# Eleven blocks of three heads, GpSimd scaling, a fixed SyncE order and a new pacing in a fused attention and gated-MLP kernel

## The chip, the cores and the metric

The kernel runs on one core of a Trainium2 chip. The metric is the device time of one execution in microseconds (us); less is better. The engines are called as the profile calls them: PE (TensorE matmul), PEld (its weight loads), DVE (VectorE), ACT (ScalarE), POOL (GpSimd) and SP (SyncE, which here only issues DMAs). Every engine works through its own instructions in a fixed order and waits on semaphores for the others.

## The reference

Input `x` has 2048 rows of 640; there are 32 heads of 20 features. All matrices are bfloat16.

```python
xn = layernorm(x)
# A: linear attention with learned softmax features
q, k, v = heads(xn @ wqkv)                     # 32 heads of 20
pq, pk = q @ w_phi, k @ w_phi                  # per head, 20 x 20
phi_q = concat(softmax(pq), softmax(-pq))      # 40 features, phi_k alike
kv = phi_k^T @ v                               # per head, summed over all rows
z  = sum over rows of phi_k
o  = (phi_q @ kv) / (phi_q . z + 1e-6)
A  = merge_heads(o) @ wo
# B: gated MLP, 1536 wide
B  = (silu(xn @ w1) * (xn @ w3)) @ w2
return x + A + B
```

No query can be finished before all 2048 keys have gone into `kv`.

## The kernel before

**Tiles.** The rows are 16 tiles of 128, grouped in 4 chunks of 512. The normalised rows of a chunk are needed transposed (`xnT`): chunk 0 is transposed on PE, chunks 1 to 3 are stored to DRAM (`xnd`) and read back by a transposing DMA, both issued by SP (`LN_out`, L363 and L368). DVE makes the normalised rows in `ln_apply` (L332).

**Units of work.** `K(t)` and `Q(t)` project a tile on PE with `wkphi` or `wqphi` (two halves of five 320-column matmuls, L424, weights folded from `wqkv` and `w_phi` by `prep`). ACT takes exponentials of both signs (L472), DVE sums them per head (L481) and takes reciprocals (L494), and DVE or POOL multiplies (L499), into a tile `phi` of 10 blocks x 2 signs x 64 columns. A block holds 64 of a tile's 640 feature columns, so it touches up to four heads. `V(t)` projects values. `KV(t)` (L542) adds a tile into two accumulators with ten matmuls of 84 columns; `kv_evac` masks off the products of different heads. `GU(c, fi)` is a gate and an up product for 128 of the 1536 MLP columns of one chunk: ten 512-column matmuls (L613), a tanh on ACT (L629), `gs` on DVE (L634), a copy on ACT (L652) and the product `hT` on POOL (L657). For queries, `phiq` goes to DRAM (L522), is read back transposed per pair of tiles as `pqT` (L534), meets `kv` in `RT(t)` (ten matmuls, L687), is divided on DVE (`ATT`, L716, L717, L722), stored (`od`, L741) and read back transposed per pair as `oT` (`OT`, L755). `O(t)` makes the output tile: 24 MLP matmuls (L780), ten with `wo` and `oT` (L786), the residual on DVE (L798) and the store (L803).

**What sets the order.** `Plan` is a list scheduler that runs when the kernel is built. Each unit of work has a planned duration and latency, the units it needs and the buffers it takes. PE's units keep the order in which they are written. For the other engines the planner takes, of the first 80 units waiting, the one that could start first:

```python
    k = (max(t, free.get(eng, 0.0)), o["n"])
```

The loop at L910 writes PE's order: tile after tile of keys, with `fill(us)` putting in as many `GU` units as the given time is worth, the remaining `Q` tiles after t = 11, and at the end eight rounds of two output tiles. Steps of a later chunk's `ln_apply` are tied to the `GU` units, one per unit (L895). The planner's order is handed on unit by unit, but the tile framework places instructions by its own priorities too, so what stands on an engine is shown below from the built programs.

**Names in short.** In this document GU1.11 is the last `GU` of chunk 1, K12 is `K(12)`, g3 and a3 are the MLP and the attention part of output tile 3.

Of the kernel before, what the change touches and what calls it, by code (L numbers as in the profile page):

```python
# [10 lines left out]
class Plan:  # L11
# [7 lines left out]
    def op(self, eng, dur, fn, deps=(), takes=None, frees=(), after=0.0, lat=0.0):  # L19
        o = dict(eng=eng, dur=dur, fn=fn, deps=[d for d in deps if d is not None], takes=takes,  # L20
                 frees=list(frees), after=after, lat=lat, n=len(self.ops), end=None, open=0)
        for f in o["frees"]:
            f["open"] += 1
        self.ops.append(o)
        return o
# [4 lines left out]
    def run(self):  # L30
# [20 lines left out]
        while left:  # L51
            best = None
            for eng, q in queue.items():
                for o in q[:1] if eng == "PE" or eng[0] == "a" else q[:80]:
# [3 lines left out]
                    k = (max(t, free.get(eng, 0.0)), o["n"])  # L58
# [3 lines left out]
            (t, _), o = best  # L62
            if o["takes"]:
                ring = self.rings[o["takes"]]
                ring.remove(min(ring))
# [12 lines left out]
def kernel(  # L78
# [30 lines left out]
    GH = 8  # L109
    EPS = 1e-5  # L110
    h0 = [64 * j // Dh for j in range(10)]
# [18 lines left out]
    pq_d = [dram.tile([256, 2 * D], bf, name=f"pqd{i}") for i in range(NST // 2)]  # L130
# [16 lines left out]
    kvm = acts.tile([P, 10, 4, Dh + 1], bf, name="kvm")  # L147
# [5 lines left out]
    def load_x(dst, t0, n, k, queue=nc.sync):  # L153
        queue.dma_start(
# [40 lines left out]
    mask = consts.tile([P, 10, 4], bf, name="mask")  # L195
# [45 lines left out]
    def kv_constants():  # L241
        for q in range(2):
            make_band(band2[64 * q : 64 * q + 64, :], 20)
        for j in range(10):
            b = 4 + 5 * h0[j] - 16 * j
            nc.gpsimd.tensor_copy(out=mask[:, j, :], in_=band2[:, b : b + 16 : 5])
# [15 lines left out]
    def act_us(n):  # L262
        return 0.075 + n / 1200.0

    def dve_us(n, x=1):
        return 0.065 + n / 960.0 / x
# [4 lines left out]
    arrive = [3.0, 3.4, 3.8, 4.2] + [19.0] * 4   # L271
# [10 lines left out]
    def ln_stats(t, k=None, parts=(0, 1)):  # L282
        c, i = divmod(t, 4)

        def fn():
# [8 lines left out]
            "DVE", 0.47 * len(parts), fn, after=arrive[t] if t < 8 else 0.0,  # L294
# [33 lines left out]
    def ln_apply(t, deps=(), k=None):  # L328
# [10 lines left out]
        apply_of[t] = plan.op("DVE", dve_us(D, 4), fn, deps=[rstd_of[t], *deps], frees=[xg_of[c]])  # L339
# [19 lines left out]
    def LN_out(c, ds):  # L359
# [3 lines left out]
            lambda: nc.sync.dma_start(out=xn_d[c][:].rearrange("(t p) d -> p t d", p=P), in_=xn[c][:]),  # L363
# [3 lines left out]
        def tr():  # L367
            pinned["xnT", c] = nc.sync.dma_start_transpose(  # L368
                out=xnT[:, :, 512 * c : 512 * c + 512], in_=xn_d[c][:]
            )  # L370

        xt = plan.op("SP", 0.5, tr, deps=[st], lat=5.0)
# [3 lines left out]
    def fetch(t, k):  # L376
# [7 lines left out]
        X_of[t] = plan.op("SP", 0.5, lambda: load_x(xg[c], i, 1, c), deps=[xg_of[c]], lat=2.5, after=30.0)  # L384
        ln_stats(t, k)
# [67 lines left out]
    def features(t, key, engines):  # L453
# [7 lines left out]
        def alp():  # L461
            box["phi"] = work.tile([P, 10, 2, 64], bf, name="phi" + key, tag="phi", bufs=5)
# [25 lines left out]
        muls = []  # L488
        for sgn, eng in enumerate(engines):

            def rec(sgn=sgn):
                if sgn == 0:
                    box["r"] = small.tile([P, 2, H], f32, name=key + "r", tag="kr", bufs=2)
                nc.vector.reciprocal(out=box["r"][:, sgn, :], in_=box["s"][:, sgn, :])  # L494

            last = plan.op("DVE", dve_us(H, 0.15), rec, deps=[last])

            def mul(sgn=sgn, eng=eng):
                ins = (nc.vector if eng == "DVE" else nc.gpsimd).tensor_mul(  # L499
                    out=box["phi"][:, :, sgn, :],  # L500
                    in0=box["e"][:, sgn, :].rearrange("p (h d) -> p h d", d=Dh),
                    in1=box["r"][:, sgn, :, None].to_broadcast([P, H, Dh]),
                )
                if key == "k" and sgn == 0:
                    pinned[t] = ins

            m = plan.op(eng, dve_us(D) if eng == "DVE" else 1.5, mul, deps=[last, pa], frees=[ea])
            if eng == "DVE":
                last = m
            muls.append(m)  # L510
        return muls, pa, box

    def K(t):
        phik_of[t], phik_a[t], _ = features(t, "k", ("DVE", "POOL"))
        pin_of[t] = phik_of[t][0]

    def Q(t, engines=("POOL", "POOL")):
# [4 lines left out]
            lambda: nc.sync.dma_start(  # L522
                out=pq_d[pair][i * P : (i + 1) * P, :], in_=box["phi"][:].rearrange("p j a f -> p (j a f)")
            ),
            deps=muls, frees=[pa], lat=2.5,
        )
        if i == 1:

            def al():
                pqT[pair] = big.tile([P, 10, 256], bf, name="pqT", tag="big")  # L530
# [3 lines left out]
                "SP", 0.5, lambda: nc.sync.dma_start_transpose(out=pqT[pair][:], in_=pq_d[pair][:]),  # L534
                deps=[pq_st[t - 1], pq_st[t], pqT_a[pair]], lat=4.5,
            )

    def KV(t):
        def fn():
            for j in (0, 5, 1, 6, 2, 7, 3, 8, 4, 9):  # L540
                acc = (kva, kvb)[j // 5]
                nc.tensor.matmul(  # L542
                    acc[:, 84 * (j % 5) : 84 * (j % 5) + 84],
                    phik_b[t][:, j, :, :].rearrange("p a f -> p (a f)"),
                    vaug[t % 4][:, h0[j] : h0[j] + 4, :].rearrange("p h d -> p (h d)"),
                    start=(t == 0 and j % 5 == 0), stop=(t == NST - 1), skip_group_check=True,
                )

        KV_of[t] = plan.op("PE", pe_us(10, 90), fn, deps=phik_of[t] + V_of[t], frees=[phik_a[t]])
# [53 lines left out]
    def GU(c, fi, mode):  # L603
# [45 lines left out]
        else:  # L649

            def uc():
# [4 lines left out]
                "POOL", 1.3,  # L656
# [7 lines left out]
    def kv_evac():  # L664
        for half, acc in enumerate((kva, kvb)):
# [343 lines left out]
```

## Time and profile before

| | |
|---|---|
| median of 6 runs | 283.35 us (282.56 to 286.35) |
| profiled execution | 284.07 us, its span 282.3 us |
| granted TensorE clock, mean | 0.988 of full speed |
| busy: PE, DVE | 269.7 us (96%), 179.9 us (64%) |
| busy: ACT, POOL | 127.7 us (45%), 123.5 us (44%) |
| DMA | 37.06 MB, 131 GB/s over the span |

The span is what the profile covers; the time of that execution is 1.77 us longer. Busy shares are means over stages with different limits. A matmul's record overlaps the next one's, so the length of a matmul is read here from the distance between two starts and not from its own duration.

### The profile page before, as it was taken

The numbers are of one execution on the slowest core, as the hardware profiler recorded it, in microseconds if no ns is written. First come the engines' busy times: TensorE is split into PE (matmuls) and PEld (weight loads), VectorE is DVE, ScalarE is ACT, GpSimd is POOL, SyncE is SP. The second block draws the span as 40 slices with busy tenths as digits, with TensorE's granted clock in tenths as the row PEclk, the third lists the DMA queues.
The fourth block names the chain that finished last, engine by engine and source line by source line (L and its number), as shares of the span: only waits on it lengthen the run. The fifth ranks groups of instructions, "written<-read, shape, count | busy, mean of one in ns | idle before, by whom it ended". The sixth has DMA issues, their size and how long they took to land.

```text
span 282.3 us, 5148 instructions
## 1 busy us (share of the span) xinstructions
PE 269.7 (96%) x1932; PEld 166.7 (59%) x1932; DVE 179.9 (64%) x367; ACT 127.7 (45%) x285; POOL 123.5 (44%) x133
## 2 busy tenths in 40 slices
PE   7999999999999995999999939999999999999996
PEld 2545555555556564565664617765766756657775
DVE  5525899998776777589689906665574564434221
ACT  3668676666677673576774211325233251130000
POOL 6233646875475454326579703336138145040000
PEclk9999999999999999799999989999999999999999
DMA  6999828700460024105735883597623675722301
GB/s 200 296 244 303 240 96 203 262 2 0 125 156 0 2 93 97 48 0 93 212 87 162 239 199 63 153 221 208 165 95 93 142 201 122 138 52 73 93 26 46
DMA packets 68217, 37.06 MB, mean 131 GB/s; under 512 B 47584, under 2 KB 66144, under 8 KB 68192
## 3 DMA queue, kind: packets, MB, share of 16 engines
q1 hardware_dynamic: 67616, 36.37, 49.1%
q10 hardware_dynamic: 576, 0.36, 0.4%
q8 instruction: 15, 0.25, 0.4%
q14 instruction: 10, 0.08, 0.1%
HBM read 12.81 MB, written 12.45 MB: 89 GB/s over the span
## 4 chain that ended last, share of the span: by engine, by line
PE 87%; DMA 7%; issue 2%; DVE 1%; ACT 1%; SPq 1%; POOL 0%; DVEq 0%; POOLq 0%; ACTq 0%
PE bank L613 35%; PE bank L424 20%; PE bank L780 18%; PE bank L786 8%; PE rtbank L687 2%; DMA xnT<-xnd_90 2%; DMA wv<-in_A_wqkv_dram 2%; DMA oT<-od_99 1%; DMA xnd_90<-xn 1%; PE bank L570 1%; PE kva L542 1%; PE kvb L542 1%; ACT eq L472 1%; DVE gs L634 0%; POOL phik L499 0%
## 5 line engine op out<-in xcount | busy, mean ns | idle before, releaser
L657 POOL TENSOR_TENSOR hT<-gs,up 128x512 bf16<-128x512 bf16 x48 | 55.2, 1156 | 59.7 <-ACT up L652 28.0
L424 PEld LDWEIGHTS <-xnT 128*128 128x128 bf16 x480 | 46.4, 99 | 25.1 <-DMA xnT<-xnd_90 3.0
L613 PE MATMUL bank<-xnT,w_108 128*128 128x512 bf16 x240 | 60.1, 379 | 0.0
L613 PE MATMUL bank<-xnT,w_107 128*128 128x512 bf16 x240 | 60.1, 380 | 0.0
L780 PE MATMUL bank<-w_109,hT 128*128 128x320 bf16 (+2 forms) x396 | 57.6, 295 | 0.0
L499 POOL TENSOR_TENSOR phiq<-eq,qr 128x640 bf16<-128x640 bf16 x27 | 34.2, 1284 | 50.6 <-issue 17.6
L634 DVE SCALAR_TENSOR_TENSOR gs<-th,bank 128x512 bf16<-128x512 bf16 x48 | 32.1, 671 | 21.4 <-ACT th L629 19.9
L780 PEld LDWEIGHTS <-hT 128*128 128x128 bf16 x396 | 37.3, 98 | 14.0
L472 ACT ACTIVATE eq<-bank 128x320 bf16<-128x320 f32 x64 | 23.0, 439 | 49.4 <-PE bank L424 49.4
L629 ACT ACTIVATE th<-bank 128x512 bf16<-128x512 f32 x48 | 28.8, 599 | 30.6 <-PE bank L613 30.2
L652 ACT ACTIVATE up<-bank 128x512 bf16<-128x512 f32 x48 | 28.7, 597 | 26.1 <-PE bank L613 25.0
L613 PEld LDWEIGHTS <-w_108 128*128 128x128 bf16 x240 | 23.2, 98 | 27.3
L613 PEld LDWEIGHTS <-w_107 128*128 128x128 bf16 x240 | 23.3, 98 | 22.9 <-issue 0.3
L481 DVE TENSOR_REDUCE qs<-eq 128x64 f32<-128x1280 bf16 x16 | 23.7, 1481 | 18.8 <-ACT eq L472 18.8
L798 DVE TENSOR_TENSOR res<-bank,xr 128x320 bf16<-128x320 f32 (+2 forms) x33 | 15.9, 482 | 30.0 <-PE bank L786 29.7
L481 DVE TENSOR_REDUCE ks<-ek 128x64 f32<-128x1280 bf16 x16 | 23.6, 1475 | 13.3 <-ACT ek L472 13.3
L786 PE MATMUL bank<-wo,oT 128*128 128x320 bf16 (+2 forms) x165 | 26.0, 305 | 4.6 <-DMA oT<-od_99 4.6
L499 POOL TENSOR_TENSOR phik<-ek,kr 128x640 bf16<-128x640 bf16 x16 | 25.2, 1575 | 10.9 <-ACT th L629 5.3
L424 PE MATMUL bank<-wkphi,xnT 128*128 128x320 bf16 x160 | 25.7, 310 | 2.8 <-DMA xnT<-xnd_90 2.8
L472 ACT ACTIVATE ek<-bank 128x320 bf16<-128x320 f32 x64 | 23.1, 439 | 6.8 <-PE bank L424 6.5
L424 PE MATMUL bank<-wv,xnT 128*128 128x320 bf16 x160 | 24.7, 299 | 0.9 <-DMA wv<-in_A_wqkv_dram 0.8
L424 PE MATMUL bank<-wqphi,xnT 128*128 128x320 bf16 x160 | 24.6, 301 | 0.0
(68 smaller groups left out, 215.5 us busy)
## 6 DMA issues: line engine op xcount, KB each, us to landing
xr<-in_A_x_dram SPq DMA_DIRECT2D x4, 640.0 KB, 4.7
out_dram<-res SPq DMA_DIRECT2D x15, 160.0 KB, 2.2
w_107<-in_B_w_dram SPq DMA_DIRECT2D x4, 480.0 KB, 6.8
w_108<-in_B_w_dram SPq DMA_DIRECT2D x4, 480.0 KB, 7.5
w_109<-in_B_w_dram SPq DMA_DIRECT2D x1, 1920.0 KB, 8.7
xg<-in_A_x_dram SPq DMA_DIRECT2D x9, 160.0 KB, 3.7
wv<-in_A_wqkv_dram SPq DMA_DIRECT2D x2, 400.0 KB, 6.2
wo<-in_A_wo_dram SPq DMA_DIRECT2D x1, 800.0 KB, 4.6
```

The costliest lines, as they stand in the source:

```text
L424: nc.tensor.matmul(o["ps"][:], xnT[:, c, t * P : (t + 1) * P], w[:, c, 320 * half : 320 * half + 320], start=(c == 0), stop=(c == KD - 1),)
L472: nc.scalar.activation(out=box["e"][:, sgn, 320 * half : 320 * half + 320], in_=o["ps"][:], func=AF.Exp, scale=1.0 - 2.0 * sgn,)
L481: nc.vector.reduce_sum(out=box["s"][:].rearrange("p a h -> p (a h)"), in_=box["e"][:].rearrange("p a (h d) -> p (a h) d", d=Dh), axis=AX.X,)
L499: ins = (nc.vector if eng == "DVE" else nc.gpsimd).tensor_mul(out=box["phi"][:, :, sgn, :], in0=box["e"][:, sgn, :].rearrange("p (h d) -> ...
L613: nc.tensor.matmul(o["ps"][:], w[:, k, fi * P : (fi + 1) * P], xs[:, k, :], start=(k == 0), stop=(k == KD - 1))
L629: nc.scalar.activation(out=box["th"][:], in_=og["ps"][:], func=AF.Tanh, scale=0.5)
L634: pinned["g", c, fi] = nc.vector.scalar_tensor_tensor(out=box["gs"][:], in0=box["th"][:], scalar=1.0, in1=og["ps"][:], op0=ALU.add, op1=AL ...
L652: nc.scalar.activation(out=box["up"][:], in_=ou["ps"][:], func=AF.Copy, scale=0.5)
L657: lambda: nc.gpsimd.tensor_mul(out=hT[c][:, fi, :], in0=box["gs"][:], in1=box["up"][:]),
L780: nc.tensor.matmul(o["ps"][:], hT[c][:, fi, ti * P : (ti + 1) * P], w2[:, fi, lo:hi], start=(fi == 0), stop=False,)
L786: nc.tensor.matmul(o["ps"][:], oT[c][:, k, ti * P : (ti + 1) * P], wo_of[0][:, k, lo:hi], start=False, stop=(k == KD - 1),)
L798: nc.vector.tensor_tensor(out=box["res"][:, lo:hi], in0=o["ps"][:], in1=xr[c][:, ti, lo:hi], op=ALU.add)
```

## The change

1. **Eleven blocks.** `phi` becomes 11 blocks of three whole heads (60 columns used of 64; the last block has two heads). The five `phi` buffers are allocated once, and POOL clears the unused columns at the start (ten memsets); the ten small copies for `mask` become one. `KV` and `RT` run eleven matmuls of 63 columns (the last 42) where they ran ten of 84. A row of `pqd` grows from 1280 to 1408 columns.
2. **Scaling.** One reciprocal for both signs in place of two. The two heads of the last block are scaled by a small DVE product (`tail`, 80 columns), and the other 30 heads by POOL, both signs. Before, DVE scaled one sign of every key tile and of the first five query tiles. Only the last key tile keeps one sign on DVE.
3. **SP's order.** Every DMA that SP issues after the opening part is chained to the one before it, so that SP keeps the planner's order. Stores of results become units of the planner. Planned times for the transposing DMAs now hold SP itself for 1.35 to 2.7 us.
4. **Spread and pacing.** `Q(0)` to `Q(6)` go one per key tile from t = 8 on; `prep` for the queries moves to t = 3 to 7. Three `ln_apply` steps per `GU` are allowed from the 21st `GU` on. The output loop is rewritten: one tile per round, g, then `RT(t + 3)`, then a, then `Q(t + 8)`, then 1.5 `GU` units up to tile 10. Planned durations of several kinds of unit are changed, and the division after `RT` gets a small preference (`soon`).

The core of the diff:

```diff
-                    k = (max(t, free.get(eng, 0.0)), o["n"])
+                    k = (max(t, free.get(eng, 0.0)) - o["soon"], o["n"])
...
+    HB = 3
+    NB = 11
+    HB_A = 6
...
+    phis = [acts.tile([P, NB, 2, 64], bf, name=f"phi{i}") for i in range(5)]
...
     def kv_constants():
+        for phi in phis:
+            nc.gpsimd.memset(phi[:, :, :, HB * Dh : 64], 0.0)
+            nc.gpsimd.memset(phi[:, NB - 1, :, 2 * Dh : HB * Dh], 0.0)
...
+        def rec():
+            box["r"] = small.tile([P, 2, H], f32, name=key + "r", tag="kr", bufs=2)
+            nc.vector.reciprocal(out=box["r"][:], in_=box["s"][:])
...
+        def tail():
+            pinned[key, t] = nc.vector.tensor_mul(
+                out=box["phi"][:, NB - 1, :, 0 : 2 * Dh].rearrange("p a (h d) -> p a h d", d=Dh),
+                in0=box["e"][:, :, n * Dh : D].rearrange("p a (h d) -> p a h d", d=Dh),
+                in1=box["r"][:, :, n:H, None].to_broadcast([P, 2, H - n, Dh]),
+            )
...
-        phik_of[t], phik_a[t], _ = features(t, "k", ("DVE", "POOL"))
+        phik_of[t], phik_a[t], _ = features(t, "k", ("POOL", "POOL" if t < NST - 1 else "DVE"))
...
-            for j in (0, 5, 1, 6, 2, 7, 3, 8, 4, 9):
-                acc = (kva, kvb)[j // 5]
+            for j in range(NB):
+                acc, at = ((kva, kvb)[j // HB_A], 63 * (j % HB_A))
...
-            for _ in range(2 if len(applies) == 2 else min(len(applies), 1)):
+            for _ in range(3 if gi >= 20 else 2 if len(applies) == 2 else 1):
...
-        if t >= 11:
-            Q(t - 11, ("DVE", "POOL"))
+        if 8 <= t < 15:
+            Q(t - 8)
...
+        if t + 3 < NST:
+            if t % 4 == 1:
+                residual(t // 4 + 1)
+            RT(t + 3)
+            ATT(t + 3)
+            OT(t + 3)
+        gates[t][1]()
+        if t + 8 < NST:
+            Q(t + 8)
+        if 3 <= t < 11:
+            fill(1.5 * 2.16)
...
+            ins = o["fn"]()
+            if o["eng"] == "SP":
+                for ins in ins:
+                    if queued is not None:
+                        order_after(ins, queued)
+                    queued = ins
```

**DVE, the last rows of chunk 3** (`xn` is a normalised tile, `gs` the gated product of one GU, `ks` and `qs` the sums of a key or query tile). Before, from the gs of GU1.11 on; the next two gs are those of GU2.0 and GU2.1:

```order
L634 SCALAR_TENSOR_TENSOR gs<-th,bank 128x512
L332 TENSOR_SCALAR xn<-xg,mv,rstd 128x640
L481 TENSOR_REDUCE ks<-ek 128x64
L634 SCALAR_TENSOR_TENSOR gs<-th,bank 128x512
L494 RECIPROCAL kr<-ks 128x32
L332 TENSOR_SCALAR xn<-xg,mv,rstd 128x640
L499 TENSOR_TENSOR phik<-ek,kr 128x10x64
L494 RECIPROCAL kr<-ks 128x32
L634 SCALAR_TENSOR_TENSOR gs<-th,bank 128x512
L332 TENSOR_SCALAR xn<-xg,mv,rstd 128x640
```

Now, from the reciprocal of K8 on; the only gs in these rows is that of GU1.11:

```order
L501 RECIPROCAL kr<-ks 128x64
L339 TENSOR_SCALAR xn<-xg,mv,rstd 128x640
L507 TENSOR_TENSOR phi_126<-ek,kr 128x2x40
L339 TENSOR_SCALAR xn<-xg,mv,rstd 128x640
L490 TENSOR_REDUCE qs<-eq 128x64
L490 TENSOR_REDUCE ks<-ek 128x64
L501 RECIPROCAL qr<-qs 128x64
L501 RECIPROCAL kr<-ks 128x64
L507 TENSOR_TENSOR phi_127<-eq,qr 128x2x40
L654 SCALAR_TENSOR_TENSOR gs<-th,bank 128x512
L507 TENSOR_TENSOR phi_123<-ek,kr 128x2x40
L339 TENSOR_SCALAR xn<-xg,mv,rstd 128x640 x2
```

The last tile of chunk 3 is now normalised behind GU1.11's gs; it stood behind GU2.1's, two GU units later.

**SP, around the first transposed attention output** (`od_99` and `od_100` are tile pairs 0 and 1 of the output, `pqd_94` is query pair 3). Before:

```order
L522 DMA pqd_94<-phiq 128x1280
L741 DMA od_99<-om 128x640
L522 DMA pqd_94<-phiq 128x1280
L741 DMA od_99<-om 128x640
L534 DMA_TRANSPOSE pqT<-pqd_94 128x10x256
L741 DMA od_100<-om 128x640
L755 DMA_TRANSPOSE oT<-od_99 128x5x256
```

Now:

```order
L879 DMA wo<-in_A_wo_dram 128x5x640
L158 DMA xr<-in_A_x_dram 128x4x640 x2
L763 DMA od_99<-om 128x640 x2
L779 DMA_TRANSPOSE oT<-od_99 128x5x256
L763 DMA od_100<-om 128x640
L540 DMA pqd_94<-phi_126 128x1408
L553 DMA_TRANSPOSE pqT<-pqd_94 128x11x256
L763 DMA od_100<-om 128x640
L832 DMA out_dram<-res 128x640
L779 DMA_TRANSPOSE oT<-od_100 128x5x256
```

The transpose of `oT` pair 0 now stands directly behind its two stores and ahead of that of query pair 3; `wo` and two residual loads (`xr`), which stood far earlier, now stand directly ahead of these stores, and a result store stands ahead of pair 1's transpose.

**POOL, two key and query tiles in the middle of the key loop** (`hT` is the product of one GU). Before, the products of Q1 with K13 and of Q2 with K14:

```order
L499 TENSOR_TENSOR phiq<-eq,qr 128x10x64
L499 TENSOR_TENSOR phik<-ek,kr 128x10x64
L657 TENSOR_TENSOR hT<-gs,up 128x512
L499 TENSOR_TENSOR phiq<-eq,qr 128x10x64
L499 TENSOR_TENSOR phik<-ek,kr 128x10x64
```

Now, those of Q0 with K9 and of Q1 with K10:

```order
L517 TENSOR_TENSOR phi_127<-eq,qr 128x10x60 x2
L517 TENSOR_TENSOR phi_123<-ek,kr 128x10x60 x2
L677 TENSOR_TENSOR hT<-gs,up 128x512
L517 TENSOR_TENSOR phi_124<-eq,qr 128x10x60 x2
L517 TENSOR_TENSOR phi_125<-ek,kr 128x10x60 x2
```

Each pair of a query and a key tile gives POOL four products in place of two, and this goes on for seven such pairs, where there were three.

More of the change, by code (lines that the diff above doesn't have):

```diff
@@ L129 @@
     xn_d = [dram.tile([512, D], bf, name=f"xnd{c}") for c in range(NSC)]
-    pq_d = [dram.tile([256, 2 * D], bf, name=f"pqd{i}") for i in range(NST // 2)]
+    pq_d = [dram.tile([256, NB * P], bf, name=f"pqd{i}") for i in range(NST // 2)]
     o_d = [dram.tile([256, D], bf, name=f"od{i}") for i in range(NST // 2)]
@@ L293, in ln_stats @@
         stats_of[t] = plan.op(
-            "DVE", 0.47 * len(parts), fn, after=arrive[t] if t < 8 else 0.0,
+            "DVE", 0.48 * len(parts) + 0.2 * (parts[-1] == 1), fn, after=arrive[t] if t < 8 else 0.0,
             deps=[X_of.get(t), pin_of.get(k)],
@@ L461, in alp @@
         def alp():
-            box["phi"] = work.tile([P, 10, 2, 64], bf, name="phi" + key, tag="phi", bufs=5)
+            box["phi"] = phis.pop(0)
+            phis.append(box["phi"])
             if key == "k":
@@ new lines, in features @@
+        last = plan.op("DVE", dve_us(2 * H, 0.15), rec, deps=[last])
+        n = HB * (NB - 1)
+        def tail():
[3 more added lines that the diff above has]
+                in1=box["r"][:, :, n:H, None].to_broadcast([P, 2, H - n, Dh]),
+            )
+        muls.append(plan.op("DVE", dve_us(2 * (H - n) * Dh), tail, deps=[last, pa], frees=[ea]))
@@ L521, in Q @@
             "SP", 0.5,
[L522 to L525, printed above, removed]
+            lambda: [
+                nc.sync.dma_start(
+                    out=pq_d[pair][i * P : (i + 1) * P, :], in_=box["phi"][:].rearrange("p b a f -> p (b a f)")
+                )
+            ],
+            deps=muls, frees=[pa], lat=2.2,
         )
@@ L938 @@
     residual(0)
-    limit = 3 * KF
-    Q(6)
-    for t in range(4):
+    for t in range(3):
+        fill(2.16)
         RT(t)
```

285 lines of the change are left out of this document (139 added, 146 removed).

## The prediction

> **What bounds the kernel now.** I read the chain of waits first, then a table of time windows, then the starts of the matmuls.
>
> ```profile
> PE 87%; DMA 7%; issue 2%; DVE 1%; ACT 1%; SPq 1%; POOL 0%; DVEq 0%; POOLq 0%; ACTq 0%
> ```
>
> PE carries 87% of the chain. The table (length, busy times, granted clock behind the counts) shows where it doesn't:
>
> ```profile
> core 0: us, PE busy (x) PEld busy (x) DVE busy (x) ACT busy (x) POOL busy (x), PEclk, DMA share, GB/s
> ...
> 109.60:116.00 6.40, 3.57 (x19) 1.93 (x17) 2.77 (x4) 1.49 (x5) 1.90 (x2) 0.73 0.31 91
> 116.00:143.70 27.70, 27.70 (x198) 17.48 (x197) 22.81 (x34) 19.74 (x49) 13.21 (x11) 1.00 0.33 78
> ...
> 162.30:170.50 8.20, 3.63 (x16) 1.93 (x15) 1.07 (x3) 0.77 (x2) 0.00 (x0) 0.79 0.88 181
> 170.50:279.40 108.90, 108.90 (x828) 73.31 (x826) 54.15 (x133) 25.17 (x54) 33.42 (x28) 1.00 0.47 120
> ```
>
> In the long windows PE is busy throughout. It stands still in two places, and there the granted clock falls too. The matmul rows give the size (start, duration, wait in brackets):
>
> ```profile
> 112.69 2.85 PE L424 MATMUL bank<-wkphi,xnT 128*128 128x320 bf16 x10 [2.83 <-DMA xnT<-xnd_90]
> 115.33 1.51 PE L613 MATMUL bank<-xnT,w_107 128*128 128x512 bf16 x5
> ...
> 121.83 1.24 PE L613 MATMUL bank<-xnT,w_107 128*128 128x512 bf16 x5
> ...
> 123.99 1.52 PE L424 MATMUL bank<-wv,xnT 128*128 128x320 bf16 x10
> ...
> 128.07 1.24 PE L613 MATMUL bank<-xnT,w_107 128*128 128x512 bf16 x5
> ...
> 140.36 0.20 PE L542 MATMUL kva<-vaug_119,phik 128*128 128x84 bf16 x1
> ...
> 140.75 1.52 PE L424 MATMUL bank<-wqphi,xnT 128*128 128x320 bf16 x10
> ...
> 144.33 0.21 PE L542 MATMUL kva<-vaug_121,phik 128*128 128x84 bf16 x1 [0.32 <-POOL phik L499]
> ...
> 167.27 2.85 PE L786 MATMUL bank<-wo,oT 128*128 128x320 bf16 x10 [4.57 <-DMA oT<-od_99]
> ```
>
> Units at full clock, from one start to the next: a GU takes 123.99 - 121.83 = 2.16 us, the three projections V, Q and K behind it 128.07 - 123.99 = 4.08, so 1.36 each, all four together 6.24, a KV 140.75 - 140.36 = 0.39.
>
> The wait for chunk 3 (K12) costs 2.83 idle, then 2.85 for a projection of 1.52 and 1.51 for half a GU of 1.24, at the lower clock, 1.6 more: **4.4 us**. The wait for the first oT costs 4.57 and, by the same surplus, **6.2 us**. KV15 waits 0.32. All that shorter waits can bring is 10.9 us; anything else must come from fewer PE columns.
>
> **The change part by part.**
>
> *Chunk 3 earlier.* From the last normalised tile the data need a store and a transpose:
>
> ```profile
> 102.68 0.44 DVE xn L332
> ...
> 103.13 3.23 DMA xnd_90<-xn
> ...
> 106.38 6.27 DMA xnT<-xnd_90
> ```
>
> This is 103.13 to 112.65, 9.5 us. Now the last tile stands behind GU1.11's gs. On DVE, K9's sums end about 2.5 after K9 does (below), then come two reciprocals (1.2), two tails and a gs (1.1, both below), two normalisations (0.44 in the row above, up to 1.2 more where POOL is in the way): 5.7 to 8.1. On SP a store of Q0's features has been put ahead of this store; POOL ends them near 5.7 (3.1 + 0.2 + 2 x 1.2, below), so it hardly delays. The chunk lands 15.2 to 17.6 us after K9's end. PE meanwhile has GU1.11, eight projections (V9, Q1, K10, V10, Q2, K11, V11, Q3), three GUs and three KVs: 2.16 + 10.9 + 6.5 + 1.0 = 20.5. Margin 2.9 to 5.3 us; the whole 4.4 goes. Chunk 2 gains margin as well, since two projections and a GU more stand between its last tile and K8.
>
> *First oT earlier.* SP's and the landing times before:
>
> ```profile
> 157.54 0.45 SPq L741 DMA_DIRECT2D od_99<-om  x1
> 159.96 2.70 SPq L534 DMA_TRANSPOSE pqT<-pqd_94  x1
> 162.71 0.57 SPq L741 DMA_DIRECT2D od_100<-om  x1
> 163.38 1.37 SPq L755 DMA_TRANSPOSE oT<-od_99  x1
> ```
>
> ```profile
> xr<-in_A_x_dram SPq DMA_DIRECT2D x4, 640.0 KB, 4.7
> ...
> wo<-in_A_wo_dram SPq DMA_DIRECT2D x1, 800.0 KB, 4.6
> ...
> od_99<-om SPq DMA_DIRECT2D x2, 160.0 KB, 3.0
> ...
> oT<-od_99 SPq DMA_TRANSPOSE x1, 3.8
> oT<-od_100 SPq DMA_TRANSPOSE x1, 4.4
> ```
>
> ```profile
> 160.65 0.17 DVE L716 TENSOR_SCALAR den<-rtbank 128x16 f32<-128x16 f32 x1 [0.29 <-PE rtbank L687]
> ...
> 161.15 0.49 DVE L722 TENSOR_TENSOR om<-rtbank,den 128x320 bf16<-128x320 f32 x1
> ```
>
> The store went out at 157.54 and landed by about 160.5, but SP was busy with query pair 3's transpose and a store until 163.38: some 2.8 us of the wait were SP's. Now that pair stands behind. The chain is division 2.0 (two halves of 160.65 to 161.64), store 3.0, transpose 3.8, issues 0.4: 9.2 us. From RT1 to a0 PE has Q7, two GUs, RT2, four MLP halves (g0, g1, 48 matmuls of 320 columns at 0.136: 6.5) and RT3: 1.36 + 4.32 + 6.5 + 0.65 = 12.8. Margin 3.6; the 6.2 go. What covers this is thinner than it looks: `wo` and two xr loads now stand just ahead of the stores. If the three run one after another from 6 us behind K15's end (when the store of Q6's features lets SP go on), they end at 6 + 4.6 + 2 x 4.7 = 20.0, a store behind them at about 21, its transpose at 25.2; a0 comes at 26. Late next are a2 and a14: from RT3 to a2 stand four projections' worth (a0, Q8, a1, Q9), g2 and two RTs, 9.4 us, against 9.2 to 9.8 (with 4.4 for the transpose, and a result store ahead of it on SP that is ready earlier). I take **+0.3** for both; 0 to 2 are possible.
>
> *KV and RT.* Ten 84-column matmuls take 0.39, ten of 320 take 1.36. That is 0.41 ns per column and 4.5 ns per matmul. Eleven with 672 columns in all: 0.326, 0.064 less, 32 times: **-2.0**. No row shows fewer than 80 columns by themselves: if a matmul took no less than 39 ns, 11 x 39 = 0.43, 0.04 more, +1.3 in all. I take the line through the rows, as the 84-column rows lie on it. A rule of the Trainium skill speaks for the other end ("TensorE: Matmul & The Clock Gate", Back-to-back issue gap): in a stream of weight loads and matmuls 128 columns take about 81 ns, so the weight load would set the pace. By it 32 matmuls more would be an estimated +2.6 us. The trace disagrees: 39 ns for 84 columns, each with its own weight load.
>
> *Scaling on POOL.* The rows that price it:
>
> ```profile
> L657 POOL TENSOR_TENSOR hT<-gs,up 128x512 bf16<-128x512 bf16 x48 | 55.2, 1156 | 59.7 <-ACT up L652 28.0 <-DVE gs L634 27.1 <-DVE kr L494 2.2
> ...
> L499 POOL TENSOR_TENSOR phik<-ek,kr 128x640 bf16<-128x640 bf16 x16 | 25.2, 1575 | 10.9 <-ACT th L629 5.3 <-DVE kr L494 4.3 <-PE bank L613 1.3
> ...
> L481 DVE TENSOR_REDUCE ks<-ek 128x64 f32<-128x1280 bf16 x16 | 23.6, 1475 | 13.3 <-ACT ek L472 13.3
> ...
> L472 ACT ACTIVATE ek<-bank 128x320 bf16<-128x320 f32 x64 | 23.1, 439 | 6.8 <-PE bank L424 6.5
> ...
> L494 DVE RECIPROCAL kr<-ks 128x32 f32<-128x32 f32 x32 | 9.5, 321 | 0.1
> ```
>
> ```profile
> 86.98 1.85 POOL L499 TENSOR_TENSOR phik<-ek,kr 128x640 bf16<-128x640 bf16 x1
> ...
> 127.98 1.27 POOL L499 TENSOR_TENSOR phik<-ek,kr 128x640 bf16<-128x640 bf16 x1
> ```
>
> ```profile
> 86.12 1.59 DVE L499 TENSOR_TENSOR phik<-ek,kr 128x640 bf16<-128x640 bf16 x1
> ...
> 125.50 0.82 DVE L499 TENSOR_TENSOR phik<-ek,kr 128x640 bf16<-128x640 bf16 x1
> ```
>
> A POOL product takes 1.27 when DVE isn't multiplying and 1.85 when it is, and DVE's own then 1.59 in place of 0.82: they wait for each other. With 600 columns that is 1.2 or 1.73, and 1.48 by the mean. DVE's products vanish save for the tails (80 columns; by the 0.82 row about 0.2 with a start-up), so I take 1.2: an iteration of V, Q, K, KV and GU gives POOL 4 x 1.2 + 1.16 + 2 x 0.2 = 6.4 us, against 6.24 + 0.33 = 6.57 on PE. POOL just keeps up. DVE has two sums (2.9), two double reciprocals (each two of 0.32, 0.6: 1.2), two tails and a gs of 512 columns (by the 0.82 row 0.7): 5.2, and waits up to 1.2 at each tail: 7.6. Reciprocals have two buffers, so DVE's next one also waits for POOL; behind it stand the gs that free PE's banks.
>
> The Trainium skill says why ("GPSIMD Engine Reference", Specifications): GpSimd shares its memory interfaces with VectorE and collides with instructions of two SBUF inputs. A tail is one; by the rule each collides, which the first rival prices. The four rows above agree.
>
> At the end of the loop this shows: K15's sums are ready 2.5 us after K15 (two exponentials and their start 1.0, one sum 1.5), the reciprocals at 3.1 and 3.7; POOL then has two products of Q6 and one of K15 (3.6), DVE two tails and one product of 600 columns (0.2, 0.2, 0.75), taken in turn: 3.1 + 4.75, ready at 7.8. PE reaches KV15 after V15, two GUs and two KVs, 1.36 + 4.32 + 0.65 = 6.3. A wait of 1.5 in place of 0.32: **+1.2** (-0.3 if POOL and DVE overlap, +3 if POOL comes late).
>
> *At no cost:*
>
> ```profile
> POOL wphi L235 <- DMA wrow<-in_A_w_phi_dram: 7.1, 1, 7.1
> ```
>
> POOL's ten memsets stand ahead of this wait for a load and fit into it; without it they would be ahead of the first weights' product. Early `prep` only changes places on PE; the reordered output tiles have the same matmuls; the larger pqT are read a whole round (g, RT, a, Q and 1.5 GU: 9.5 us) or more after their transposes go out.
>
> **Sum.** -4.4 - 6.2 + 0.3 + 1.2 - 2.0 = -11.1, so 284.07 - 11.1 = 273.0 for an execution like the profiled one. That one stands 0.7 above the median of 283.35, from which the sum gives 272.3; I say **272.5**. Own range: 270 (no new waits, -1.5) to 275.
>
> **The rivals.**
> 1. *POOL and DVE pace the key loop.* At 1.48 a product, 4 x 1.48 + 1.16 = 7.08 against 6.57: 0.51 late in each of seven iterations, 3.6, all of it due at KV15, with the clock surplus of 1.6 since PE then stands about 5 us. 272.5 + 5.2 = 277.7. For it: the 86.98 row. Against: the 127.98 row.
> 2. *The loads ahead of the first stores keep a0 waiting.* Margin 0.8 if they run in series; 2 us late plus clock is +3.5: 276.
> 3. *Block count and not columns sets KV and RT*: +1.3 for -2.0, 275.8. The TensorE page's 81 ns is this rule.
> 4. *Slower: SP's chain holds every pair's transpose.* A result store waits for DVE ahead of each oT transpose. For pairs 2 to 6 a chain of 9 us has 14 to 19 us of PE work as cover; it decides when the chain passes that by 2 us in seven pairs (14 us). At 2.5 us, 17.5: 290. Against: the results wait only for the attention part of earlier tiles.
> 5. *The waits only move*: chunk 3 or oT late elsewhere by as much; about 283.
>
> **How the numbers follow.** Forecast 0.64, rivals 0.15, 0.08, 0.07, 0.03 and 0.03. The range 269.5 to 277 takes in the forecast's range, rivals 2 and 3 and half of rival 1's price. About 1% is what a measurement of this kernel can tell from no change. Faster by over 1%: 0.64 + 0.15 + 0.08 + 0.07 = 0.94; within 1% 0.03; slower 0.03.
>
> **What would show it.** Right: no PE wait on xnT or oT above 1 us, granted clock full from 15 us to the end, KV at 0.32, POOL products near 1.2, one PE wait of 1 to 2 us at KV15. Wrong: POOL products of 1.5 and a long wait at KV15 (rival 1); PE waiting for oT behind `wo` or xr (2); KV of 0.43 (3); SP waiting for results with PE waiting for oT in round after round (4).

## The result, and the profile after

| | before | after |
|---|---|---|
| median | 283.17 us (20 runs) | 274.31 us (10 runs) |
| ratio after to before, 95% interval | | 0.9705 (0.967 to 0.9739) |
| profiled execution, its span | 284.07, 282.3 us | 274.03, 272.3 us |
| granted clock, mean | 0.988 | 1.0 |

Faster, as forecast, and inside the range of 269.5 to 277. The forecast time of 272.5 was 1.8 us too good; against the profiled execution, for which the sum was made, 273.0 stands beside 274.03.

The chain of waits of the changed kernel, by engine. PE carried 87% of it before. That its share fell is no loss of PE's, which is busy for 97% of the span (96% before): it means that another engine, mostly DVE, now stands in the chain that ended last.

```profile
PE 77%; DVE 13%; issue 4%; DMA 2%; ACT 2%; SPq 0%; ACTq 0%; DVEq 0%
```

The table of windows (columns as in the prediction). The stretch of K12 and that of the first oT, which had 3.57 us of PE in 6.40 and 3.63 in 8.20, are full, with the clock at 1.00. So is the one that ends at 162.30, in which a0 now starts. Only the stretch of 116.00, which was full, lacks 0.95 us.

```profile
109.60:116.00 6.40, 6.40 (x52) 4.12 (x50) 4.96 (x8) 4.46 (x11) 6.34 (x7) 1.00 0.73 193
116.00:143.70 27.70, 26.75 (x218) 16.66 (x217) 25.82 (x31) 18.11 (x45) 24.29 (x21) 1.00 0.40 109
143.70:162.30 18.60, 18.60 (x150) 11.53 (x149) 10.98 (x33) 6.22 (x12) 8.18 (x8) 1.00 0.62 188
162.30:170.50 8.20, 8.20 (x77) 6.07 (x76) 7.35 (x15) 2.89 (x8) 2.31 (x2) 1.00 0.74 180
```

PE's rows in the places that matter (start, duration, wait in brackets). K12 (at 114.44) and a0 (161.19) wait for nothing now. KV15 waits, and three GU wait for `gs` of an earlier GU, which frees their PSUM bank:

```profile
48.68 1.24 PE L633 MATMUL bank<-xnT,w_107 128*128 128x512 bf16 x5 [0.80 <-DVE gs L654]
...
53.52 1.24 PE L633 MATMUL bank<-xnT,w_107 128*128 128x512 bf16 x5 [0.51 <-DVE gs L654]
...
107.07 1.24 PE L633 MATMUL bank<-xnT,w_107 128*128 128x512 bf16 x5 [0.76 <-DVE gs L654]
...
114.44 1.52 PE L432 MATMUL bank<-wkphi,xnT 128*128 128x320 bf16 x10
...
132.46 0.35 PE L562 MATMUL kva<-vaug_118,phi_124 128*128 128x63 bf16 x6
132.65 0.31 PE L562 MATMUL kvb<-vaug_118,phi_124 128*128 128x63 bf16 x5
132.80 1.52 PE L432 MATMUL bank<-wqphi,xnT 128*128 128x320 bf16 x10
...
142.98 0.35 PE L562 MATMUL kva<-vaug_121,phi_125 128*128 128x63 bf16 x6 [0.94 <-DVE phi_125 L517]
...
161.19 1.52 PE L811 MATMUL bank<-wo,oT 128*128 128x320 bf16 x10
```

The bracket shows the idle time that the profile gives to the releaser. From matmul start to matmul start, less the usual spacing, the three GU lose 0.96, 0.67 and 0.92 us, 2.55 in all, and KV15 1.11. In the same measure the kernel before lost nothing at those GU and 0.49 at KV15.

SP's rows: the store of chunk 3's last rows and its transpose, the loads `wo` and xr, the first pair's output transpose, and query pair 3's transpose behind it. Below them the time from issue to landing: of chunk 3's transpose, from the view of DMAs, and of the eight output transposes, from the view of the tile oT.

```profile
101.75 0.37 SPq L370 DMA_DIRECT2D xnd_90<-xn  x1
105.00 2.75 SPq L375 DMA_TRANSPOSE xnT<-xnd_90  x1
...
141.49 0.39 SPq L879 DMA_DIRECT2D wo<-in_A_wo_dram  x1
141.93 1.32 SPq L158 DMA_DIRECT2D xr<-in_A_x_dram  x2
...
151.95 1.32 SPq L779 DMA_TRANSPOSE oT<-od_99  x1
...
159.37 3.16 SPq L553 DMA_TRANSPOSE pqT<-pqd_94  x1
```

```profile
xnT<-xnd_90 SPq DMA_TRANSPOSE x1, 4.8
```

```profile
DMA to landing us min/median/max: 3.5/3.8/4.1
```

So chunk 3 lands at 109.8, 4.6 us ahead of K12, and the first oT by 156.1 at the latest (151.95 + 4.1), 5.1 ahead of a0. The loads in front of the first stores cost nothing here: the first store, issued behind them, took 4.2 us to land (2.5 before), but the second, issued 2.5 us after it, took 2.1 and still landed last.

DVE's rows at two of the late `gs`, and POOL's beside them:

```profile
46.34 0.90 DVE L507 TENSOR_TENSOR phi_125<-ek,kr 128x80 bf16<-128x80 bf16 x1
47.17 0.88 DVE L294 BATCH_NORM_STATS2 stats<-xg 128x6 f32<-128x320 bf16 x2
47.96 0.66 DVE L654 SCALAR_TENSOR_TENSOR gs<-th,bank 128x512 bf16<-128x512 bf16 x1
...
99.16 2.56 DVE L339 TENSOR_SCALAR xn<-xg,mv,rstd 128x640 bf16<-128x640 bf16 x2
...
105.31 1.11 DVE L507 TENSOR_TENSOR phi_124<-eq,qr 128x80 bf16<-128x80 bf16 x1
106.34 0.68 DVE L654 SCALAR_TENSOR_TENSOR gs<-th,bank 128x512 bf16<-128x512 bf16 x1
```

```profile
45.99 1.16 POOL L677 TENSOR_TENSOR hT<-gs,up 128x512 bf16<-128x512 bf16 x1 [0.91 <-DVE gs L654]
...
99.10 2.44 POOL L517 TENSOR_TENSOR phi_123<-ek,kr 128x600 bf16<-128x600 bf16 x2
...
105.12 2.36 POOL L517 TENSOR_TENSOR phi_124<-eq,qr 128x600 bf16<-128x600 bf16 x2 [2.38 <-ACT eq L481]
```

POOL's product of 600 columns takes 1.2, as forecast. But a tail of 80 columns on DVE takes 0.90 and 1.11 us, and it ends within 0.12 us of the POOL product beside it: 46.34 + 0.90 = 47.24 against 47.15, 105.31 + 1.11 = 106.42 against 106.30 (half of the pair). The two normalisations end with POOL's two products, at 101.7 against 101.54. I read this as DVE being held by POOL, with `gs` behind it; e4 and e7 below test it.

**The account of the 10.0 us between the two spans**, from the starts of the matmuls: K12 -4.5; first oT -6.25; KV and RT -1.4; KV15 +0.6; the three GU +2.55; the start -0.7. That is -9.7; 0.3 is spread over the rest.

### The profile page after: what moved, and what is told of

Read it like the earlier page. It is cut to its first block, busy times and chain, and to the rows that moved or that the text cites. A ratio compares the mean times of both kernels' runs of the same rounds, so it can differ in the third digit from the quotient of the medians.

```text
span 272.3 us, 5218 instructions
## 1 busy us (share of the span) xinstructions
PE 264.1 (97%) x1964; PEld 163.9 (60%) x1964; DVE 184.7 (68%) x347; ACT 126.9 (47%) x285; POOL 138.8 (51%) x154
## 4 chain that ended last, share of the span: by engine, by line
PE 77%; DVE 13%; issue 4%; DMA 2%; ACT 2%; SPq 0%; ACTq 0%; DVEq 0%
PE bank L633 30%; PE bank L798 19%; PE bank L432 16%; PE bank L811 8%; DVE xn L339 2%; DVE ks L490 2%; PE rtbank L708 2%; DVE gs L654 2%; DMA wv<-in_A_wqkv_dram 2%; DVE qs L490 2%; DVE stats L294 1%; PE bank L590 1%; DVE kr L501 1%; ACT ek L481 1%; DVE phi_124 L507 1%
## 5 line engine op out<-in xcount | busy, mean ns | idle before, releaser
L677 POOL TENSOR_TENSOR hT<-gs,up 128x512 bf16<-128x512 bf16 x48 | 56.0, 1169 | 77.1 <-DVE gs L654 35.2
L432 PEld LDWEIGHTS <-xnT 128*128 128x128 bf16 x480 | 45.8, 98 | 21.1 <-ACT xnT L418 1.1
L798 PE MATMUL bank<-w_109,hT 128*128 128x320 bf16 (+2 forms) x396 | 55.0, 295 | 0.0
L798 PEld LDWEIGHTS <-hT 128*128 128x128 bf16 x396 | 38.2, 98 | 15.6
L811 PE MATMUL bank<-wo,oT 128*128 128x320 bf16 (+2 forms) x165 | 24.6, 294 | 0.0
L432 PE MATMUL bank<-wkphi,xnT 128*128 128x320 bf16 x160 | 24.3, 299 | 0.0
L737 DVE TENSOR_SCALAR den<-rtbank 128x18 f32<-128x18 f32 (+1 forms) x32 | 4.9, 173 | 27.8 <-PE rtbank L708 27.8
L825 DVE TENSOR_TENSOR res<-bank,xr 128x320 bf16<-128x320 f32 (+2 forms) x33 | 14.6, 472 | 10.4 <-PE bank L811 10.4
L811 PEld LDWEIGHTS <-oT 128*128 128x128 bf16 x165 | 14.9, 97 | 4.9
```

The source lines that it names most:

```text
L432: nc.tensor.matmul(o["ps"][:], xnT[:, c, t * P : (t + 1) * P], w[:, c, 320 * half : 320 * half + 320], start=(c == 0), stop=(c == KD - 1),)
L677: lambda: nc.gpsimd.tensor_mul(out=hT[c][:, fi, :], in0=box["gs"][:], in1=box["up"][:]),
L798: nc.tensor.matmul(o["ps"][:], hT[c][:, fi, ti * P : (ti + 1) * P], w2[:, fi, lo:hi], start=(fi == 0), stop=False,)
L811: nc.tensor.matmul(o["ps"][:], oT[c][:, k, ti * P : (ti + 1) * P], wo_of[0][:, k, lo:hi], start=False, stop=(k == KD - 1),)
L825: nc.vector.tensor_tensor(out=box["res"][:, lo:hi], in0=o["ps"][:], in1=xr[c][:, ti, lo:hi], op=ALU.add)
```

## The experiments

The kernels, each with its ratio to the kernel before on the same chip:

| run | edit | median us | ratio (95%) | span |
|---|---|---|---|---|
| e1 | after, first oT behind query pair 3 | 283.12 | 0.9972 (0.9938 to 1.0005) | 280.4 |
| e2 | after, old pacing | 285.48 | 1.0061 (1.0026 to 1.0095) | 283.4 |
| e3 | after, a key product on DVE | 288.01 | 1.0149 (1.0093 to 1.0205) | 285.6 |
| e4 | after, tails on POOL | 272.16 | 0.9594 (0.9545 to 0.9643) | 270.4 |
| e5 | after, Q6 behind KV13 | 273.02 | 0.9644 (0.9606 to 0.9681) | 271.3 |
| e6 | e4 and e5 together | 270.59 | 0.958 (0.9533 to 0.9626) | 268.3 |
| e7 | after, normalisation with a sum | 273.88 | 0.9676 (0.9633 to 0.9719) | 272.3 |
| e8 | after, fewer KV columns | 273.58, one run | | 271.9 |
| e9 | before, new pacing alone | 278.92 | 0.9846 (0.9763 to 0.9929) | 277.3 |
| e10 | before, oT ahead of pqT alone | 281.92 | 0.9969 (0.9929 to 1.001) | 282.0 |

**e1: the order of SP undone.** A chain of its matmuls holds PE's order as the changed kernel has it, while the edit changes SP's.

```diff
         if t == 1:
             Q(7)
+            oT_of[0]["deps"].append(pqT_of[3])
```

> The changed kernel, with the first pair's output transpose put behind query pair 3's transpose on SyncE again, as before; PE's order is held as it was. My theory: SyncE is busy with the query transpose from 159.4 to 162.5 in the changed kernel, the output transpose then lands at 165.9 in place of 155, and the first attention part, due at 161.2, waits 4.7 us and pays some 1.6 us of halved clock: 280 to 281 us. Rival (the wait only moved, the order of SyncE buys nothing): 274 to 275 us.

SP's rows and PE's (with the chain, all matmuls have the line of the chaining function):

```profile
159.43 3.16 SPq L553 DMA_TRANSPOSE pqT<-pqd  x1
162.72 0.49 SPq L763 DMA_DIRECT2D od<-om  x1
163.74 3.03 SPq L779 DMA_TRANSPOSE oT<-od  x2
```

```profile
167.85 2.85 PE L1019 MATMUL bank<-wo,oT 128*128 128x320 bf16 x10 [6.47 <-DMA oT<-od]
```

The wait is there, 1.8 us longer than expected, in part since a store got between the two transposes. With the halved clock the span is 8.1 us longer than the changed kernel's, and the time 2 us above my bounds. In the changed kernel the order of SP is needed.

**e2: the pacing undone.** PE's order is held here too.

```diff
-            for _ in range(3 if gi >= 20 else 2 if len(applies) == 2 else 1):
+            for _ in range(2 if len(applies) == 2 else 1):
```

> The changed kernel, with the normalised tiles paced as before: one with each gate step, two when two are left. PE's order is held as it was. My theory: the last tile comes 12 to 13 us later on VectorE, chunk 3 lands near 123 in place of 109.8, and K12, due at 114.4, waits some 8.5 us and pays 1.6 of clock; from it go the waits that the four tiles now cause near 106 (0.9) and at KV15 (1.1): 281 to 284 us. Rival (the pacing was worth what K12 waited before and no more): 278.5 to 279 us. Rival (K12 has cover either way): 274 us.

```profile
123.48 2.85 PE L1018 MATMUL bank<-wkphi,xnT 128*128 128x320 bf16 x10 [9.86 <-DMA xnT<-xnd]
```

Chunk 3 lands at 123.4. K12 waits 9.86, and the clock is halved for 10.2 us, 4.2 of them after PE has started again. The GU near 106 no longer waits, but KV15 still waits its 1.1 us, which I had expected to go. So the main step is my theory's, with 11.1 us of span above its bounds. The old pacing costs more in the new order than it did in the old one: the last tile is normalised at 114.5, where it stood at 102.6 in the kernel before. That the features now crowd the steps to which the tiles are tied is my reading of it; no run isolates it.

**e3: a key product back on DVE.**

```diff
-        phik_of[t], phik_a[t], _ = features(t, "k", ("POOL", "POOL" if t < NST - 1 else "DVE"))
+        phik_of[t], phik_a[t], _ = features(t, "k", ("DVE", "POOL"))
```

> The changed kernel, with the first of each key tile's two products (600 columns) on VectorE, as before; GpSimd has three products for each iteration of the key loop in place of four. My theory: VectorE and not GpSimd is the tighter of the two (5.9 us of 6.5 in an iteration without normalisations), and a product of 0.8 to 1.8 us more makes it late: the waits for the gates grow, 276 to 280 us. Rival (GpSimd's four products make the wait at KV15 and hold VectorE up): 272.5 to 273.5 us.

DVE's product and the `gs` behind it, then PE's rows:

```profile
114.36 1.78 DVE L517 TENSOR_TENSOR phi<-ek,kr 128x600 bf16<-128x600 bf16 x1
116.06 0.67 DVE L654 SCALAR_TENSOR_TENSOR gs<-th,bank 128x512 bf16<-128x512 bf16 x1
```

```profile
57.96 3.27 PE L633 MATMUL bank<-xnT,w 128*128 128x512 bf16 x9 [2.86 <-DVE gs L654]
...
116.79 1.91 PE L633 MATMUL bank<-xnT,w 128*128 128x512 bf16 x5 [3.11 <-DVE gs L654]
...
156.24 0.35 PE L562 MATMUL kva<-vaug,phi 128*128 128x63 bf16 x6 [3.40 <-DVE phi L517]
```

The direction is my theory's, the size is some three times it. DVE's product takes 1.52 us by the mean, POOL's only 1.2: DVE comes second and waits (above, at 114.36 against 114.30 for POOL's). All waits of PE that were not in the startup sum to 13.1 us against 3.7 in the changed kernel, and two of them halve the clock. So DVE and not POOL is the engine without slack here, and to scale all on GpSimd is not a detail: in the new order it is worth 13 us of span.

**e4: the tails on POOL.** The exponentials get a 33rd head of zeros, and one product covers all eleven blocks.

```diff
-        muls.append(plan.op("DVE", dve_us(2 * (H - n) * Dh), tail, deps=[last, pa], frees=[ea]))
...
-                    out=box["phi"][:, 0 : NB - 1, sgn, 0 : HB * Dh].rearrange("p b (h d) -> p b h d", d=Dh),
+                    out=box["phi"][:, :, sgn, 0 : HB * Dh].rearrange("p b (h d) -> p b h d", d=Dh),
```

> The changed kernel without VectorE's tails: the two last heads are scaled by GpSimd's product, over 33 heads of which the last is zero (660 columns, some 1.32 us in place of 1.2). My theory: the three waits of PE for a gate's tile (near 48, 53 and 106, 2.55 us in all) come from VectorE being held in the tails (0.64 to 1.24 us each for 80 columns) while GpSimd multiplies; without them they go for the most part, and KV15 waits no longer: 271.5 to 273 us. Rival (VectorE is late from sums and normalisations alone, and GpSimd's 5.3 + 1.16 us of products fill the 6.5 us of an iteration): 274 to 276 us, with the wait at KV15 longer.

The groups by line, and PE's only wait after the startup that is longer than 0.3 us (at KV15):

```profile
L515 POOL TENSOR_TENSOR phi<-e,r 128x660 bf16<-128x660 bf16 x63 | 82.0, 1323 | 19.5 <-DVE res L823 10.1 <-DVE r L508 3.8 <-issue 3.0
```

```profile
141.07 0.36 PE L560 MATMUL kva<-vaug,phi 128*128 128x63 bf16 x6 [1.15 <-POOL phi L515]
```

The three waits for `gs` are gone: my theory, and the cause of the 2.55 us is shown. Half of the rival is right as well: KV15, where I expected no wait, waits no less, and now for POOL. Sums and normalisations were left as they were, and every `gs` is in time: they alone were not too much for DVE.

**e5: query tile 6 behind KV13.**

```diff
-        if 8 <= t < 15:
+        if 8 <= t < 14:
             Q(t - 8)
+        if t == 15:
+            Q(6)
```

> The changed kernel, with the projection and features of query tile 6 moved from ahead of K15 to behind KV13 on PE, and so behind K15's products on GpSimd and VectorE. My theory: KV15's wait (1.1 us) is the time of Q6's two products, which stand ahead of K15's; it goes, and the projection of 1.36 us stands between as cover: 273.0 to 273.4 us, no wait at KV15. Rival (GpSimd is late by its whole backlog, whatever the order): the wait stays, 274 to 275 us.

KV15's row:

```profile
141.97 0.35 PE L562 MATMUL kva<-vaug,phi 128*128 128x63 bf16 x6
```

KV15 waits for nothing; the three GU wait as before the edit (0.96, 0.67 and 0.93). The edit also puts Q6's projection between K15 and KV15, but this cover of 1.36 us isn't what did it: K15's products are done 5.5 us after K15's end, in place of 7.3, and KV15 would be due at 6.35 without Q6 in between. The wait at KV15 was Q6's two products ahead of K15's, not POOL's whole backlog.

**e6: both.**

> The tails on GpSimd (as in e4) and query tile 6 behind KV13 (as in e5) together. My theory: the waits of e4 and e5 are different ones, so both go: 270.5 to 271.2 us, and no wait of PE above 0.5 us between 15 us and the end. Rival (GpSimd, with products of 660 columns, is late at KV15 in any order): 272 us, with the wait at KV15 left.

The chain of waits of this kernel:

```profile
PE 95%; DMA 2%; issue 1%; SPq 0%; ACT 0%; DVE 0%
```

No wait of PE above 0.3 us is left after the startup. The two waits were independent: its span is 4.0 us shorter than the changed kernel's, and the two waits (2.55 and 1.1) with 0.2 of the startup make 3.85. The median of 270.59 us is the lowest of all, and its interval lies apart from that of the change, though not from those of e4 and e5.

**e7: the normalisation in a form that also gives a sum.** I take it that in this form the second operation belongs to the sum, so that the kernel leaves out the division by the standard deviation; no run shows that by itself. The number of normalisations and their sizes are the same, and each is followed by a short read of the sum (0.08 us).

```diff
-                op0=ALU.subtract, op1=ALU.mult,
+                op0=ALU.subtract, op1=ALU.mult, accum_out=junk[:, t : t + 1],
```

> The changed kernel, with the normalisation written in the form that also gives the sum of its outputs. My theory: the 0.44 to 1.32 us of a normalisation are 0.4 of work and a wait for GpSimd's product in the fast mode; the form with the sum runs in the slow mode at some 0.75 us each, whether GpSimd multiplies or not, and the wait near 106 (0.9) shrinks by the half: 273.8 to 274.3 us. Rival (it is GpSimd's products that slow any VectorE instruction): 1.3 us for those beside a product, and 274.3 to 276 us.

All sixteen by line, durations in ns as least, median and most; then the same row of the changed kernel:

```profile
L340 DVE TENSOR_SCALAR_CACHE_REDUCE xn<-xg,mv,rstd x16: 839/928/940, 4.7 to 100.3; 128x640 bf16<-128x640 bf16 x16
```

```profile
L339 DVE TENSOR_SCALAR xn<-xg,mv,rstd x16: 387/636/1325, 4.6 to 100.4; 128x640 bf16<-128x640 bf16 x16
```

The form with the sum takes 0.84 to 0.94 everywhere, also beside POOL's products; the usual one takes 0.39 alone and up to 1.325 beside them. So the long normalisations were a wait for POOL, and not every DVE instruction meets it. The GU near 106 no longer waits, and the first of the three waits 0.35 in place of 0.96; the time is the same within the interval, because what the gates gain (2.55 us of waits became 1.03) this form, longer where POOL is idle, loses ahead of the first transposes: before 15 us PE loses 6.0 us in place of 4.4.

**e8: KV with fewer columns.**

```diff
-                hs = slice(HB * j, min(HB * j + HB, H))
+                hs = slice(HB * j, min(HB * j + (HB if t == 0 else 1 + t % 2), H))
```

> The changed kernel, in which the KV matmuls of all key tiles but the first leave out columns: one head of three (21 columns) for even tiles, two heads (42 columns) for odd ones; the sums over keys lack the rest. Line of the forecast (0.41 ns a column and 4.5 ns a matmul): 21.7 ns for 42 columns and 13 for 21, so 0.24 and 0.15 us a KV in place of 0.343. Rival (from some width down the time of a matmul with its own weight load no longer falls; the 42-column matmuls of the changed kernel already take 29 ns): 0.31 to 0.32 us for both.

PE's rows of an odd tile and of an even one; the distance to the Q behind it is the KV's time:

```profile
96.32 0.31 PE L562 MATMUL kva<-vaug,phi 128*128 128x42 bf16 x6
96.47 0.28 PE L562 MATMUL kvb<-vaug,phi 128*128 128x42 bf16 x5
96.60 1.52 PE L432 MATMUL bank<-wqphi,xnT 128*128 128x320 bf16 x10
...
102.83 0.30 PE L562 MATMUL kva<-vaug,phi 128*128 128x21 bf16 x6
102.98 0.27 PE L562 MATMUL kvb<-vaug,phi 128*128 128x21 bf16 x5
103.11 1.52 PE L432 MATMUL bank<-wqphi,xnT 128*128 128x320 bf16 x10
```

0.28 us for both, where my line gave 0.24 and 0.15. A matmul with its own weights took no less than 0.28 / 11 = 25.5 ns, so the line through the 84 and 320-column rows doesn't go on below that; the rival is right that there is a floor, though it is lower than it said. The Trainium skill names it ("TensorE: Matmul & The Clock Gate", "Wait — 56ns, not 53.3ns?"): start to start never drops below about 25 ns. The trace agrees. The change's 63 columns, at 31 ns, are still above it.

**e9 and e10: one part of the change alone, in the kernel before.** e9 has the new rule of e2's diff. PE's order follows, since the placement had moved work ahead of the late K12.

> The kernel before with nothing but the new pacing of the normalised tiles (up to three with a gate step from the 21st on). My theory: the wait of K12 (2.83 us and the halved clock, 4.4 in all) goes, since chunk 3 lands some 5 us earlier and more, and nothing takes its place: 278.5 to 279.5 us. Rival (the crowded normalisations make VectorE late for the gates, as near 106 in the changed kernel): 280 to 282 us.

278.92, as my theory had it, and K12 waits for nothing: the pacing alone is some 4.4 us, half of the result (by its interval 2 to 6.7 us).

e10 ties query pair 3's transpose behind the first oT:

```diff
+    def transposed(key, pair, ins):
+        pinned[key, pair] = ins
+        if key == "q" and pair == 3:
+            order_after(ins, pinned["o", 0])
```

> The kernel before with nothing but SyncE's order changed: the first pair's output transpose ahead of query pair 3's transpose. My theory: the order alone gives back only the 2.8 us in which SyncE was busy with the query transpose; the rest of the first attention part's wait (4.6 us) came from there being too little work of PE ahead of it, which the change's 48 matmuls of the MLP moved ahead supply: a wait of about 1.9 us is left, 278.9 to 280.6 us (with or without the halved clock). Rival (the order of SyncE is the whole of it): 277 us and no wait.

```profile
160.66 1.25 SPq L762 DMA_TRANSPOSE oT<-od  x1
...
162.64 3.43 SPq L540 DMA_TRANSPOSE pqT<-pqd  x1
```

```profile
164.57 2.85 PE L794 MATMUL bank<-wo,oT 128*128 128x320 bf16 x10 [3.47 <-DMA oT<-od]
```

The transpose goes out 2.7 us earlier and a0 starts 2.7 earlier, as expected. But the placement of instructions, with oT earlier, put a0 ahead of a projection, so a0 was due 1.6 earlier; and the wait fell so that the clock was halved for 6.8 us in place of 3.4. In the end 282.0 of span for 282.3, a ratio whose interval reaches 1, and a time above my 278.9 to 280.6. So as built, the order alone buys next to nothing in the kernel before, and without it (e1) the changed kernel loses 8 us. That the PE work moved ahead of a0 is needed too is argued from the 3.47 us of wait that are left here, 1.6 of which come from a0's new place; no run takes that work alone out of the changed kernel.

## Why the prediction was right, and where its sizes were off

1. **Chunk 3 earlier: right, with some luck.** It lands 16.8 us after K9's end (93.0), within 15.2 to 17.6; the margin is 4.6, within 2.9 to 5.3. 4.4 were forecast, 4.5 came, and e9 has about the same by itself. But two errors offset each other in the 16.8: the last tile is normalised 8.7 us after K9's end, where 5.7 to 8.1 were forecast (point 6 says why), and store and transpose took 8.1 in place of 9.5. And 0.92 of the margin is the wait of the GU near 106.
2. **First oT earlier: right.** 6.2 forecast, 6.25 came; the margin is at least 5.1 rather than 3.6, mostly because the division took 1.5 in place of 2.0 and the later store 2.1 in place of 3.0. e1 shows that SP's order is needed; that the PE work ahead of a0 is needed as well fits e10 but isn't shown by itself. The loads of rival 2 didn't decide it, though they came near: the first store landed only 0.4 us ahead of the second.
3. **a2 and a14: +0.3 forecast, 0 came.** No PE row waits for oT in any round, so rival 4 didn't come either.
4. **KV and RT: the step was right, the size was not.** 2.0 forecast, 1.4 came: a KV takes 0.343 and not 0.326. The last block's 42 columns take 29 ns and not the line's 21.7; the rest is a nanosecond for each of the other ten. Rival 3 was wrong here: it needed 39 ns for each matmul, 63 columns took 31, and e8 finds the floor at 25.
5. **KV15: right mechanism, +0.6 for +1.2.** It starts 7.5 us after K15's end, 7.8 were forecast, and the KV of before gave 0.49 by the same measure. e5 shows that Q6's two products ahead of K15's are the cause.
6. **Scaling on POOL: the term that was mis-sized.** "A POOL product takes 1.27 when DVE isn't multiplying" held, 1.2 for 600 columns, and rival 1 with 1.48 was wrong. But the step read the collision as something that both share, and rival 1, which was to price it, put it on POOL's products alone. What the tails cost DVE was counted as "waits up to 1.2 at each tail", and set against PE only in the iteration of the key loop and at KV15; at the gates it got nothing. In the runs POOL loses next to nothing and DVE pays: 0.64 to 1.27 us for nearly every tail that the step had at 0.2, 1.28 for a normalisation. Where a `gs` stood behind it, PE's next bank was late: 2.55 us. Without the tails all of it goes (e4), without the long normalisations 1.5 of it (e7).
7. **At no cost:** no wait of PE on the memsets or the larger pqT shows. The earlier start (0.7 us) was not forecast. The first projection starts at 6.89 in the changed kernel and at 7.59 in the one before; in e1 to e6, with the same startup or nearly so, PE loses 4.25 to 5.0 us before 15 us, against 4.4 in the changed kernel and 5.1 before, so it is scatter for the most part: luck, which brought the measured time nearer to the sum.

In sum: the GU +2.55, KV15 -0.6, KV and RT +0.6, a2 and a14 -0.3, the start -0.7 and K12 and oT -0.15 make 1.4 us. The sum missed 1.0; the rest is, but for rounding, the 0.3 that the account above leaves spread.

Why a collision costs the one and not the other is told by the Trainium skill ("SBUF — State Buffer", "Who interferes with whom"): VectorE and GpSimd share a pair of ports, which the instruction that starts first holds to its end; VectorE needs it for two inputs in SBUF or in a fast mode of one input, and not for a sum. The runs agree: the tails (two inputs) and the normalisations (one input) end with POOL's product, the form with the sum (e7) doesn't wait, and the sums of queries and keys take 1.43 to 1.49 throughout. In the kernel before, DVE's product began first (86.12 against 86.98) and POOL's took 1.85; in the changed one POOL's is already running and takes 1.2.

## What to carry to other kernels

- When two engines hold each other up, price the collision at the one that starts second, and ask what stands behind it: here 80 columns on VectorE cost up to 1.27 us, and the work behind them freed a bank for PE. Giving GpSimd 10% more work (1.32 for 1.2 us) was the cheaper way.
- The worth of a transfer moved ahead in its queue can hang on the rest of the order: here 8 us in the changed kernel and next to nothing by itself. An edit that undoes one half shows the need, an edit that does one half alone shows what it is worth.
- Before a backlog is blamed for a wait at the end of a loop, look at the order within it: moving one tile's work behind the last key tile took the whole wait away.

## What the runs showed of the hardware

**The clock is decided in fixed stretches of 3.41 us, not by the length of a wait.** In every trace the stretches of full and of halved clock in its clock record begin and end on a grid of that width: in the kernel before at 112.45 and 167.06, 16 x 3.413 apart, each 3.41 long; 6.83 in e1 (a wait of 6.5), 10.24 in e2 (9.9). In e3 a wait of 3.11 halved the clock and the longer one of 3.40 did not. Its windows, the wait of 116.79 in the first and that of 156.24 in the second (the clock behind the counts):

```profile
112.00:122.00 10.00, 6.84 (x30) 3.33 (x29) 10.00 (x12) 3.48 (x9) 6.52 (x6) 0.83 0.80 137
...
152.00:158.00 6.00, 2.55 (x21) 1.25 (x21) 5.55 (x8) 1.19 (x3) 6.00 (x5) 1.00 0.80 208
```

By PE's busy time in windows laid on the grid, the first wait left 0.88 of one stretch idle; the second fell on two, 0.56 and 0.45 of which were idle. In all the runs, a stretch at full clock that was idle for 0.61 (e7, at its end) or more is followed by a halved one, and none with 0.56 or less is. A halved stretch that was idle for 0.30 was followed by another (e10), one with 0.16 was not (e1). The Trainium skill has the window ("TensorE: Matmul & The Clock Gate", "What's actually happening": 3413 ns, free-running); the trace agrees. So the surplus of 1.6 us that the prediction put on each long wait depends on where the wait falls on the grid. The executions of the kernel before that stand on record scatter in step with this: those with a mean clock of 0.994 (one such stretch in 282 us) took 280.0 to 282.6 us, with 0.988 (two) 282.8 to 284.8, with 0.982 (three) 283.6 to 285.6 and with 0.976 (four) 285.6 to 285.9. The changed kernel has hardly a long wait left, and nearly all of its executions ran at 0.999 or 1.0.
